# Seven products instead of eight for one more group of second products, with one block's products moved to the end

## The chip, the cores and the metric

One core of one Trainium2 chip runs the kernel. The metric is the time of the program on the device in microseconds (us), smaller being better. A profile of one execution tells, per engine, when each instruction began and how long it took.

## The reference, cut to what matters

```python
def chain(q, k, v, w_gate, w_val, w_out, rms_g, w_in, w_out2):   # names shortened
    a = decayed_linear_attention(q, k, v)      # 2 x 8 heads x 768 tokens x 64
    x = a.transpose(0, 2, 1, 3).reshape(1536, 512)
    xn = x / sqrt(mean(x * x, -1) + 1e-6) * rms_g
    g, val = xn @ w_gate, xn @ w_val           # 512 -> 1536
    x2 = (silu(g) * val) @ w_out               # 1536 -> 512   first layer
    h = x2 @ w_in                              # 512 -> 2048
    return maximum(0.01 * h, h) @ w_out2       # 2048 -> 512   second layer
```

The weights come as 64-bit floating point numbers and the rest in 32 bits.

## The kernel before, in words

**Data.** After the attention part the 1536 tokens lie in three blocks of 512 (0, 1, 2). Features run over the partitions in slabs of 128. The first layer has 12 slabs of hidden features, worked on in three groups of four (`G1`, groups 0 to 2); the second has 16, in four groups of four (`G2`, groups 3 to 6). A group makes its first products (`g` and `v`, or `i`), turns them into gated values, and multiplies these by its second weights (`o`, or `p`); the sums of the second products are kept across groups.

**A product** of fp32 accuracy is made of three products of rounded parts (high times high, high times low, low times high). So a slab's product with one block is 12 matmuls of 512 columns. Every value that enters a matmul needs a high part (a copy on ScalarE, ACT) and a low part (a subtraction on VectorE, DVE). A weight slab is first turned from 64-bit numbers into fp32 by four VectorE steps (L466, L470, L475, L484), then split (L487 on ACT, L491 on DVE).

**Sevens.** A pair of slabs and the blocks 1 and 2 form a two-by-two product. The kernel makes it with seven half products of sums and differences in place of eight. For the first products this is `quad` (7 steps of 6 matmuls, for a pair of slabs); for the second products it is `seventh`. It works on sums of gated values (`follow`, L741) and on sums of weights (L425, split at L432), and adds the result of each of the seven kinds to the kept sums with two VectorE additions (L807). The kinds run in the order 1, 5, 6, 3, 7, 2, 4. Block 0 is always multiplied plainly: `whole` for first products, `down` for second ones.

**Which groups.** `SEVEN = 4` names the four groups of the second layer, `SEVEN1 = (1,)` the first layer's middle group. In groups 0 and 2 the second products are plain: `down` for each slab and block, 12 matmuls each, and at a block's end `evac1` adds four banks to the kept sums.

**The kept sum of block 0** has no room in the fast memory while its tile (`extra()`, called `more` in the profile) holds gated values: `evac1` writes it with four GpSimd DMAs to `held` and, in group 1, reads it back with four more (L698).

**The turn to the second layer.** Group 2 ends with block 0, then block 1, then the four `down` steps of block 2. After a block the result is split into parts (`x2_parts`), and the sums over blocks 1 and 2 that the sevens of `i` need are made by `sums_of` (four differences, four high parts, four low parts, each over 1024 columns). These operations wait in the list `sums`, from which two are taken behind each step. `HEAD = "dddd0"` orders the beginning of group 3: four `down` steps, one `whole`, then the quads.

**Order and room.** `plan` writes the steps out in the order of TensorE; `run` walks them with a planner that gives VectorE and ACT assumed costs and puts weight conversions where it sees time, latest when a step needs the weight. Converted weight slabs take one of 14 places (`UNITS = 12` and `UNITS2 = 2`); a sum of two slabs takes two. A place is given back after the last product that reads it. Behind the hand-ordered attention part the framework orders each engine's queue by this order and by what is ready. Weights are loaded through SP's queue, three raw slabs ahead.

Of the kernel before, what the change touches and what calls it, by code (L numbers as in the profile page):

```python
# [8 lines left out]
F32 = mybir.dt.float32  # L9
# [3 lines left out]
AF = mybir.ActivationFunctionType  # L13
# [19 lines left out]
SEVEN1 = (1,)  # L33
HEAD = "dddd0"
# [29 lines left out]
def chain_kernel(ctx: ExitStack, tc: tile.TileContext, qk_t, kv, w1, w2, mask, qdec, kdec, sdec, rms_g, ident, out):  # L64
# [585 lines left out]
    def down(gi, f, b):  # L650
        kinds, fs = groups[gi]
        L = kinds[-1]
        key = (L, f, b)
        upper(key)
        lower(key)
        accumulate(L, gi, f, b, f == fs[0], f == fs[-1], L == "o" or b > 0)
        used(f"{L}{f}")
        if f == fs[-1]:
            banks = acc.pop("b")
            first = gi in (0, len(G1))  # L660
            by_copy = gi in (0, len(G1)) or b == 0 and gi not in (len(G1) - 1, len(groups) - 1)
            later.append(("a" if by_copy else "v", 2.4, lambda: (evac1 if L == "o" else evac2)(gi, b, banks)))
        placed[0] = order.index(key) + 1

    def evac1(gi, b, banks):
        last = gi == len(G1) - 1
        if b:
            if gi == 0:
                acc[b] = xp.tile([P, 4, 512], F32, tag=f"acc{b}", name=f"x2acc{b}")
            for m in range(4):  # L670
                dst = acc[b][:, m, :]
                if gi == 0:
                    nc.scalar.activation(out=dst, in_=banks[m], func=AF.Copy)
                else:
                    nc.vector.tensor_tensor(out=dst, in0=banks[m], in1=dst, op=ALU.add)
            if not last:
                return
            highs, lows = ([lambda m=m, do=do: do(m) for m in range(2 * b - 2, 4)] for do in x2_parts(b))
            if b == 1:
                sums.extend(highs + lows)  # L680
                return
            one, two = slice(0, 2), slice(2, 4)
            ops = sums_of(acc, x2h, x2l, acc[1][:, one], acc[1][:, two], x2h[2][:, one], x2l[2][:, one], extra()[:, two])
            both = [lambda i=i: [ops[n]() for n in (f"{i}", f"h{i}")] for i in range(4)]
            sums.extend(both[:2] + [ops["l1"]] + highs + [ops["l0"]] + lows + [both[2], ops["l2"], both[3], ops["l3"]])
            return
        acc[0] = extra()
        for m in range(4):
# [5 lines left out]
            if gi == 0:  # L694
                nc.gpsimd.dma_start(out=held[m], in_=t)
            else:
                nc.gpsimd.dma_start(out=held[m], in_=t, accum_op=ALU.add)
                nc.gpsimd.dma_start(out=t, in_=held[m])  # L698
        if last:
            high, low = x2_parts(0)  # L700
            sums.extend([lambda m=m, do=do: do(m) for do in (high, low) for m in range(4)])

# [53 lines left out]
    def seventh(gi, n, f):  # L756
# [44 lines left out]
        def put():  # L801
            for m in range(2):
# [3 lines left out]
                else:  # L806
                    nc.vector.tensor_tensor(out=dst, in0=banks[m], in1=dst, op=ALU.add)  # L807
            if gi == len(groups) - 1 and LAST[b, row] == n:
# [236 lines left out]
    def plan():  # L1045
# [12 lines left out]
        for gi, (kinds, fs) in enumerate(groups):  # L1058
# [19 lines left out]
            if first:  # L1078
                for n in HEAD:
                    if n == "d":  # L1080
                        fill.pop(0)()
                    else:
                        f = fs[int(n)]
                        put((f"i{f}",), lambda f=f: whole("i", f, 0, x2h, x2l))
# [9 lines left out]
            elif gi in seven:  # L1094
                for f in fs[::2]:
                    own = [fill.pop(0) for _ in range(min(2, len(fill)))]
# [4 lines left out]
                wholes = [lambda f=f: put((f"i{f}",), lambda: whole("i", f, 0, x2h, x2l)) for k, f in enumerate(fs) if not first or str(k) not in HEAD]  # L1101
# [241 lines left out]
```

## Time and profile before

| | |
|---|---|
| time, median of 3 runs | 580.07 us (580.04 to 580.52) |
| span of the profiled execution, first to last instruction | 578.7 us |
| busy TensorE (PE) / VectorE (DVE) / ScalarE (ACT) / GpSimd (POOL) | 569.6 / 516.4 / 361.8 / 39.3 us |
| matmuls | 3098 |

The profiled execution is told by its span; 1.4 us of the median lie outside it. An engine's busy time is the time in which at least one of its instructions ran. Instructions of one engine overlap in the profile: on VectorE an operation that is shown with 0.68 us can be followed 0.6 us after its start. L612 is line 612 of the kernel shown above.

### The profile page before, as it was taken

To read this page: it belongs to the slowest core of one execution; us is meant where nothing else is said; L and a number is where in the kernel's file an instruction comes from. 1 tells how busy PE (TensorE), PEld (TensorE's weight loads), DVE (VectorE), ACT (ScalarE), POOL (GpSimd) and SP (SyncE) were. 2 spreads that over 40 slices of the span, in tenths; PEclk is the share of its full clock that TensorE was granted. 3 is DMA by queue.
4 is the path that set the end of the run, shared out by engine and by line. 5 is a ranking of instruction groups with operands and counts; after the bars stand their busy time and mean duration, and the time that the engine had idled before them with its cause. 6 is when DMAs were issued, how large, how long until landed. Compare 5 with 4: busy or idle time off the path is not lost.

```text
span 578.7 us, 8510 instructions
## 1 busy us (share of the span) xinstructions
PE 569.6 (98%) x3098; PEld 470.1 (81%) x3098; DVE 516.4 (89%) x950; ACT 361.8 (63%) x666; POOL 39.3 (7%) x48
## 2 busy tenths in 40 slices
PE   8899999999999999999999999999999999999997
PEld 5788788887888888888888878888888888888886
DVE  5899999999577999999588999999999999997793
ACT  2789656776565455675464567778756785676330
POOL 2332100010000000030000000000100020002100
PEclk9999999999999999999999999999999999999999
DMA  8991240435022201484410111213511363011545
GB/s 336 408 386 61 74 143 3 143 117 178 1 72 74 72 2 36 117 199 170 133 57 18 37 36 37 72 40 108 182 37 37 109 151 73 33 36 24 123 81 139
DMA packets 34922, 60.13 MB, mean 104 GB/s; under 512 B 19392, under 2 KB 19776, under 8 KB 34880
## 3 DMA queue, kind: packets, MB, share of 16 engines
q1 hardware_dynamic: 31728, 52.24, 28.0%
q0 software_dynamic: 3008, 7.34, 5.5%
q8 instruction: 24, 0.39, 0.3%
q14 instruction: 18, 0.15, 0.1%
q10 hardware_dynamic: 144, 0.00, 0.0%
HBM read 51.19 MB, written 8.39 MB: 103 GB/s over the span
## 4 chain that ended last, share of the span: by engine, by line
PE 81%; DVE 8%; DMA 6%; ACT 3%; issue 1%; SPq 0%; POOL 0%; DVEq 0%; ACTq 0%; POOLq 0%
PE ao L612 10%; PE X L776 9%; PE iX L974 8%; PE ap L612 8%; PE i L581 8%; PE Z L776 7%; PE v L581 6%; PE g L581 6%; PE gX L974 4%; PE iZ L974 4%; PE vX L974 4%; PE gZ L974 2%; DMA qkv<-in_qk_t 2%; PE vZ L974 2%; PE iY L974 2%; DMA qkv<-in_kv 2%
## 5 line engine op out<-in xcount | busy, mean ns | idle before, releaser
L612 PE MATMUL ap<-w_p,gp_0h 128*128 128x512 f32 (+1 forms) x130 | 39.6, 386 | 0.0
L581 PE MATMUL i<-x2h,w_i 128*128 128x512 f32 x128 | 31.8, 390 | 0.0
L581 PE MATMUL g<-xh,w_g 128*128 128x512 f32 x128 | 31.8, 391 | 0.0
L581 PE MATMUL v<-xh,w_v 128*128 128x512 f32 x128 | 31.7, 390 | 0.0
L612 PE MATMUL ao<-go_0h,w_o 128*128 128x512 f32 x96 | 31.5, 390 | 0.0
L612 PEld LDWEIGHTS ap<-w_p,gp_0h 128*128 128x128 f32 x130 | 24.4, 188 | 5.0
L581 PEld LDWEIGHTS g<-xh,w_g 128*128 128x128 f32 x128 | 24.0, 188 | 5.1 <-issue 0.2
L581 PEld LDWEIGHTS i<-x2h,w_i 128*128 128x128 f32 x128 | 24.0, 188 | 5.0
L581 PEld LDWEIGHTS v<-xh,w_v 128*128 128x128 f32 x128 | 24.0, 188 | 4.9
L612 PE MATMUL ap<-w_p,gp_0l 128*128 128x512 f32 (+1 forms) x65 | 25.1, 386 | 0.0
L912 ACT ACTIVATE more<-i 128x512 f32<-128x512 f32 x16 | 9.5, 594 | 21.5 <-PE i L581 21.5
L612 PEld LDWEIGHTS ao<-go_0h,w_o 128*128 128x128 f32 x96 | 18.0, 188 | 3.7
L612 PE MATMUL ao<-go_2h,w_o 128*128 128x512 f32 x64 | 20.6, 391 | 0.1
L612 PE MATMUL ao<-go_1h,w_o 128*128 128x512 f32 x64 | 20.4, 390 | 0.0
L974 PE MATMUL iZ<-x2h,w_si 128*128 128x512 f32 x64 | 20.3, 391 | 0.0
L974 PE MATMUL iX<-th,w_si 128*128 128x512 f32 x64 | 19.8, 391 | 0.0
L612 PE MATMUL ao<-go_0l,w_o 128*128 128x512 f32 x48 | 18.7, 389 | 0.0
L538 ACT ACTIVATE wb_i<-raw_i 128x512 int32<-128x512 uint32 x16 | 10.8, 673 | 11.2 <-DVE wa_p L484 3.9
L581 PE MATMUL v<-xl,w_v 128*128 128x512 f32 x64 | 17.2, 392 | 0.0
L581 PE MATMUL g<-xl,w_g 128*128 128x512 f32 x64 | 17.2, 391 | 0.0
L197 DVE TENSOR_TENSOR a<-sc,mask_sb 128x1024 f32<-128x1024 f32 (+1 forms) x13 | 14.6, 1137 | 3.0 <-PE sc L185 2.6
L581 PE MATMUL i<-x2l,w_i 128*128 128x512 f32 x64 | 17.1, 390 | 0.0
(366 smaller groups left out, 1776.5 us busy)
## 6 DMA issues: line engine op xcount, KB each, us to landing
raw_i<-in_w SPq DMA_DIRECT2D x16, 512.0 KB, 3.8
raw_p<-in_w SPq DMA_DIRECT2D x16, 512.0 KB, 3.7
raw_g<-in_w SPq DMA_DIRECT2D x12, 512.0 KB, 4.1
raw_v<-in_w SPq DMA_DIRECT2D x12, 512.0 KB, 3.8
raw_o<-in_w SPq DMA_DIRECT2D x12, 512.0 KB, 3.6
qkT<-in_qk_t SPq DMA_DIRECT2D x7, 512.0 KB, 6.6
kv<-in_kv SPq DMA_DIRECT2D x7, 512.0 KB, 8.1
out<-more POOLq DMA_DIRECT2D x12, 256.0 KB, 4.2
```

Source lines behind the costliest of these rows:

```text
L197: nc.vector.tensor_tensor(out=s["a"][:, j], in0=s["sc"][:, j], in1=mask_sb[:, j], op=ALU.mult)
L538: nc.scalar.activation(out=m, in_=low.bitcast(U32), func=AF.Copy, scale=2.0 ** -29)
L581: nc.tensor.matmul(out=dst, lhsT=lhs, rhs=rhs, start=(n == 0), stop=(n == len(pairs) - 1), skip_group_check=True)
L612: nc.tensor.matmul(out=acc["b"][m][:, c:c + cut], lhsT=lhs, rhs=rhs[:, c:c + cut], start=(start and n == 0), stop=(stop and n == 2), skip_ ...
L776: nc.tensor.matmul(out=acc[side][m], lhsT=lhs, rhs=rhs, start=(start and f == fs[0] and k == 0), stop=(f == fs[-2] and k == 2), skip_group ...
L912: nc.scalar.activation(out=a, in_=x, func=AF.Prelu, alpha=0.01)
L974: nc.tensor.matmul(out=dst, lhsT=lhs, rhs=rhs, start=(start and n == 0), stop=(n == 5), skip_group_check=True)
```

## The change

The second products of group 2 are made as sevens too (`SEVEN1 = (1, 2)`), for blocks 1 and 2. Their weights `o8` to `o11` are converted behind all of the group's `g` and `v`, and two pairs of weight sums are made for them. Block 0's gated values of the group go into `extra()`, so the kept sum stays in `held` one group longer: the read-back of its slab m moves out of `evac1` into `down`, behind the making of the parts of the slab that lay there. Block 0's four `down` steps come behind the sevens, and then the quads of `i` begin without a `whole` ahead of them; block 0's four `whole` steps of group 3 go two into its second quad and two among its sevens. The parts of blocks 1 and 2 and their sums are taken up as soon as the last of the seven kinds for a half of a block is added (`x2_sums`, called from `seventh`); `sums_of` is called without a spare tile.

```diff
--- before.py
+++ after.py
@@ -30,8 +30,7 @@
 COST_SUM = {n: ("a", 0.54) if n in "Hh" else ("v", 0.34 if n in "1234" else 0.6) for n in "123H4hLl"}
 TWICE = "gvi"
 SEVEN = 4
-SEVEN1 = (1,)
-HEAD = "dddd0"
+SEVEN1 = (1, 2)
 RAWS = 3
 WARM = 7
 LOADS = "q0 k0 m g s k1 q1 d q2 q3 k2 k3 q4 k4 q5 w w q6 w q7 k6 k8 k7 k5 i q8 q9 k9 q10 k10"
@@ -653,6 +652,9 @@
         key = (L, f, b)
         upper(key)
         lower(key)
+        if gi == len(G1) - 1:
+            m = f - fs[0]
+            nc.gpsimd.dma_start(out=extra()[:, m, :], in_=held[m])
         accumulate(L, gi, f, b, f == fs[0], f == fs[-1], L == "o" or b > 0)
         used(f"{L}{f}")
         if f == fs[-1]:
@@ -665,24 +667,9 @@
     def evac1(gi, b, banks):
         last = gi == len(G1) - 1
         if b:
-            if gi == 0:
-                acc[b] = xp.tile([P, 4, 512], F32, tag=f"acc{b}", name=f"x2acc{b}")
+            acc[b] = xp.tile([P, 4, 512], F32, tag=f"acc{b}", name=f"x2acc{b}")
             for m in range(4):
-                dst = acc[b][:, m, :]
-                if gi == 0:
-                    nc.scalar.activation(out=dst, in_=banks[m], func=AF.Copy)
-                else:
-                    nc.vector.tensor_tensor(out=dst, in0=banks[m], in1=dst, op=ALU.add)
-            if not last:
-                return
-            highs, lows = ([lambda m=m, do=do: do(m) for m in range(2 * b - 2, 4)] for do in x2_parts(b))
-            if b == 1:
-                sums.extend(highs + lows)
-                return
-            one, two = slice(0, 2), slice(2, 4)
-            ops = sums_of(acc, x2h, x2l, acc[1][:, one], acc[1][:, two], x2h[2][:, one], x2l[2][:, one], extra()[:, two])
-            both = [lambda i=i: [ops[n]() for n in (f"{i}", f"h{i}")] for i in range(4)]
-            sums.extend(both[:2] + [ops["l1"]] + highs + [ops["l0"]] + lows + [both[2], ops["l2"], both[3], ops["l3"]])
+                nc.scalar.activation(out=acc[b][:, m, :], in_=banks[m], func=AF.Copy)
             return
         acc[0] = extra()
         for m in range(4):
@@ -695,10 +682,28 @@
                 nc.gpsimd.dma_start(out=held[m], in_=t)
             else:
                 nc.gpsimd.dma_start(out=held[m], in_=t, accum_op=ALU.add)
-                nc.gpsimd.dma_start(out=t, in_=held[m])
         if last:
             high, low = x2_parts(0)
             sums.extend([lambda m=m, do=do: do(m) for do in (high, low) for m in range(4)])
+
+    x2_ops = {}
+
+    def x2_sums(b, row):
+        one, two = slice(0, 2), slice(2, 4)
+        high, low = x2_parts(b)
+        ms = range(2 * row, 2 * row + 2)
+        own = [lambda m=m, do=do: do(m) for do in (high, low) for m in ms]
+        if b == 2 and not row:
+            return []
+        if b == 2:
+            return own
+        if not row:
+            x2_ops.update(
+                sums_of(acc, x2h, x2l, acc[1][:, one], acc[1][:, two], x2h[2][:, one], x2l[2][:, one])
+            )
+        both = [lambda i=i: [x2_ops[n]() for n in (f"{i}", f"h{i}")] for i in range(4)]
+        lows = [lambda i=i: x2_ops[f"l{i}"]() for i in range(4)]
+        return own + (both[3:] + lows[3:] if row else both[:3] + [lows[2], lows[0], lows[1]])
 
     def x2_parts(b):
         if b not in x2h:
@@ -805,6 +810,8 @@
                     nc.scalar.activation(out=dst, in_=banks[m], func=AF.Copy)
                 else:
                     nc.vector.tensor_tensor(out=dst, in0=banks[m], in1=dst, op=ALU.add)
+            if gi == len(G1) - 1 and LAST[b, row] == n:
+                sums.extend(x2_sums(b, row))
             if gi == len(groups) - 1 and LAST[b, row] == n:
                 t = units.tile([P, 2, 16, 32], F32, tag="u", name=f"turned{b}_{row}")
                 for m in range(2):
@@ -1076,12 +1083,8 @@
             fill = downs(groups[gi - 1][1], 0 if gi - 1 in seven else 2, gi - 1) if gi else []
             first = gi == len(G1)
             if first:
-                for n in HEAD:
-                    if n == "d":
-                        fill.pop(0)()
-                    else:
-                        f = fs[int(n)]
-                        put((f"i{f}",), lambda f=f: whole("i", f, 0, x2h, x2l))
+                while fill:
+                    fill.pop(0)()
             if gi in seven and L == "o":
                 wholes = [lambda n=n, f=f: put((f"{n}{f}",), lambda: whole(n, f, 0, xh, xl)) for f in fs for n in kinds[:-1]]
                 for f in fs[::2]:
@@ -1092,13 +1095,15 @@
                             if i7 in BEHIND[2] and own:
                                 own.pop(0)()
             elif gi in seven:
+                wholes = [lambda f=f: put((f"i{f}",), lambda: whole("i", f, 0, x2h, x2l)) for f in fs]
                 for f in fs[::2]:
+                    if first and f > fs[0]:
+                        fill, wholes = wholes[:2], wholes[2:]
                     own = [fill.pop(0) for _ in range(min(2, len(fill)))]
                     for i7, (keys, step) in enumerate(quad("i", f)):
                         put(keys, step)
                         if i7 in BEHIND[2] and own:
                             own.pop(0)()
-                wholes = [lambda f=f: put((f"i{f}",), lambda: whole("i", f, 0, x2h, x2l)) for k, f in enumerate(fs) if not first or str(k) not in HEAD]
             if gi in seven:
                 for n, more in zip((1, 5, 6, 3, 7, 2, 4), (1, 0, 1, 0, 1, 0, 1)):
                     for f in fs[::2]:
```

## Rows read from the trace of the kernel before

**Rows 1.** The page, busy time of each engine over the span, instructions behind the x.
```profile
PE 569.6 (98%) x3098; PEld 470.1 (81%) x3098; DVE 516.4 (89%) x950; ACT 361.8 (63%) x666; POOL 39.3 (7%) x48
```
**Rows 2.** The page, VectorE's busy tenths in 40 slices of 14.5 us.
```profile
DVE  5899999999577999999588999999999999997793
```
**Rows 3.** Waits of TensorE over the span: total us, times, longest (longest row).
```profile
PE sc L185 <- DMA qkv<-in_qk_t: 2.3, 3, 1.0
```
**Rows 4.** The chain from 290 us: start, us, what.
```profile
300.83 2.72 PE ao L612 x12
```
**Rows 5.** Timeline of TensorE at the turn of blocks 1 and 2: start, us, instruction.
```profile
323.56 0.39 PE L612 MATMUL ao<-go_1h,w_o 128*128 128x512 f32 x1
324.08 0.47 PE L612 MATMUL ao<-go_2h,w_o 128*128 128x512 f32 x1
```
**Rows 6.** VectorE's groups by shape, 315 to 337 us: count, busy us, mean ns.
```profile
L675 DVE TENSOR_TENSOR x2acc<-ao,x2acc 128x512 f32<-128x512 f32 x8 | 5.1, 686 | 0.0
```
**Rows 7.** The same view, 174 to 232 us, the first layer's second group.
```profile
L807 DVE TENSOR_TENSOR x2acc<-X,x2acc 128x512 f32<-128x512 f32 x8 | 5.2, 682 | 0.0
L807 DVE TENSOR_TENSOR x2acc<-Z,x2acc 128x512 f32<-128x512 f32 x6 | 4.0, 684 | 0.0
...
L432 DVE TENSOR_TENSOR w_so<-wa_o,w_so 128x512 fp32r<-128x512 f32 x4 | 2.7, 684 | 0.0
L425 DVE TENSOR_TENSOR wa_o<-wa_o,wa_o 128x256 f32<-128x256 f32 x6 | 2.5, 420 | 0.1
...
L741 DVE TENSOR_TENSOR gs<-gs,gs 128x512 f32<-128x512 f32 x2 | 1.4, 688 | 0.0
```
**Rows 8.** Timeline of VectorE around the second layer's first sevens.
```profile
358.73 0.42 DVE L425 TENSOR_TENSOR wa_p<-wa_p,wa_p 128x256 f32<-128x256 f32 x1
359.06 0.68 DVE L741 TENSOR_TENSOR is<-iu,is 128x512 f32<-128x512 f32 x1
359.67 0.42 DVE L425 TENSOR_TENSOR wa_p<-wa_p,wa_p 128x256 f32<-128x256 f32 x1
...
363.73 0.68 DVE L432 TENSOR_TENSOR w_sp<-wa_p,w_sp 128x512 fp32r<-128x512 f32 x1
```
**Rows 9.** Busy time of VectorE by stretch: stretch and length, busy (instructions).
```profile
234.00:255.00 21.00, 20.52 (x43) 1.00 0.58 153
255.00:364.50 109.50, 97.05 (x169) 1.00 0.24 77
364.50:421.00 56.50, 56.31 (x108) 1.00 0.31 103
421.00:520.00 99.00, 97.95 (x187) 1.00 0.25 70
```
**Rows 10.** Timeline of TensorE, first product of the sevens' third kind, group 3.
```profile
365.25 0.39 PE L776 MATMUL X<-gq_6h,w_sp 128*128 128x512 f32 x1
```
**Rows 11.** Timeline of VectorE, the last weight sum of group 4.
```profile
419.79 0.69 DVE L432 TENSOR_TENSOR w_sp<-wa_p,w_sp 128x512 fp32r<-128x512 f32 x1
```
**Rows 12.** Timeline of TensorE, the same third kind of product, group 4.
```profile
422.37 0.39 PE L776 MATMUL X<-gq_6h,w_sp 128*128 128x512 f32 x1
```
**Rows 13.** VectorE's groups by shape, 404 to 420.3 us.
```profile
L475 DVE SCALAR_TENSOR_TENSOR wa_i<-raw_i,wa_i 128x512 int32<-128x512 int32 x2 | 1.4, 684 | 0.0
...
L470 DVE TENSOR_SCALAR wa_i<-wa_i 128x512 int32<-128x512 int32 x2 | 0.8, 420 | 0.0
L466 DVE TENSOR_SCALAR wa_i<-wa_i 128x512 f32<-128x512 f32 x2 | 0.8, 419 | 0.0
...
L484 DVE CUSTOM_DVE_ANT_0 wa_i<-wa_i,wb_i 128x1024 uint16<-128x1024 uint16 x1 | 0.7, 683 | 0.0
```
**Rows 14.** Timeline of TensorE, first product with the weights of group 5.
```profile
444.13 0.62 PE L974 MATMUL iX<-x2h,w_i 128*128 128x512 f32 x2
```
**Rows 15.** Timeline of VectorE, in brackets the idle time before and its releaser.
```profile
288.63 0.69 DVE L922 TENSOR_TENSOR g<-v,g 128x512 f32<-128x512 f32 x1 [6.08 <-PE v L581]
```
**Rows 16.** Timeline of TensorE, start of the products of the first layer's last group.
```profile
231.31 0.61 PE L974 MATMUL gX<-xh,w_g 128*128 128x512 f32 x2
```
**Rows 17.** Timeline of GpSimd, the first read-back of a kept sum.
```profile
256.89 0.58 POOL L698 DMA_DIRECT2D more<-held  x1 [2.74 <-DVE wa_o L470]
```
**Rows 18.** DMA issues: count, KB each, median us from issue to landing.
```profile
more<-held POOLq DMA_DIRECT2D x4, 256.0 KB, 5.4
```

## Prediction

> **What bounds the kernel now.** I read the page first. TensorE is busy for 98% of the span and VectorE for 89% [rows 1]; but the slices show VectorE at 9 tenths from about 300 to 520 us with hardly a break [rows 2]. Two engines are near their limit, so the next view is who waits. TensorE's list of waits is short: five entries, the largest of 2.3 us in three pieces, all at lines of the attention part [rows 3]. In the two layers TensorE simply runs: twelve matmuls take 2.72 us [rows 4], 0.2267 us each, and the same step shows everywhere. The one visible hitch near the change is at the turn from block 1 to block 2: two matmuls that should start 0.23 us apart start 0.52 us apart [rows 5], so 0.3 us is lost.
>
> So the time is the number of matmuls, as long as VectorE keeps up. How near it is to not keeping up is read in two ways. First its idle time: 0.5 us in 234 to 255 us, 12.45 us in 255 to 364.5, 0.2 us in 364.5 to 421, and 1.05 us in the 99 us after that [rows 9]. Second, how long before its use a weight is ready. The last weight sum for group 3's sevens ends at 364.4 us [rows 8]; the product that needs it is in the second half of the kind that starts at 365.25 [rows 10], and it reads the low part eight matmuls later, at 367.1. The lead is 2.7 us. In group 4 the last one ends at 420.5 [rows 11] and is needed at 422.37 + 1.81 = 424.2 [rows 12], a lead of 3.7 us.
>
> **The change part by part.**
>
> *Matmuls.* Plain, blocks 1 and 2 cost 4 slabs x 2 blocks x 12 = 96 matmuls; as sevens 2 pairs x 7 x 6 = 84. Twelve go: -2.7 us [rows 4]. The turn from block 1 to block 2 goes too, and its hitch with it: -0.3 us [rows 5]. That is -3.0 us on the engine that sets the end.
>
> *VectorE.* What it does more of is seen in group 1, which works this way already. Its price per operation is the distance of two starts, 0.33 us for 256 columns and 0.61 us for 512 [rows 8]; the shown durations, 0.42 and 0.68, would count the overlap twice. Weight sums: eight of 256 columns and four low parts [rows 7], 8 x 0.33 + 4 x 0.61 = 5.1 us. Low parts of the gated sums: 14 in place of 8, 3.7 us. Differences at L741: 4 per pair, 8 in all, the line in [rows 7] standing for four such lines of two: 4.9 us. Additions to the kept sums: 14 [rows 7] in place of 8 [rows 6], 3.7 us. Together 17.3 us (19.8 if the durations counted). Block 0's additions, x2's parts and the sums over blocks are as many as before.
>
> *ACT.* Six more high parts and four for weight sums; it is busy for 361.8 us of 578.7 [rows 1] and hides them.
>
> *Where VectorE can put 17.3 us.* The idle time from 234 to 364.5 us is 12.9 us, to 421 us 13.1 us [rows 9]. If all of it can be used, group 3's last weight sum comes 17.3 - 12.9 = 4.4 us later, at 368.8, while TensorE wants it at 367.1 - 0.3 = 366.8 (the twelve matmuls saved are spent on one more `whole` ahead of this point): 2.0 us late. Group 4's comes 4.2 us later, at 424.7, and is wanted at 424.2 - 3.0 = 421.2: 3.5 us late. But not all that stands ahead of it is as urgent: before it VectorE had already done seven steps on the weights of group 5 [rows 13], 4 x 0.33 + 3 x 0.61 = 3.2 us, and these are first used at 444.13 [rows 14]. If they give way, 0.3 us of stall is left. So the stall is between 0.3 and 3.5 us. I take 1.0, nearer the low end, because those seven steps are for later weights and the order of work follows the order of need.
>
> *Idle time that can't be used.* Of the 12.9 us, 6.1 us is one wait [rows 15], ending with a product of TensorE: VectorE had run ahead as far as the 14 places let it. After the change the second weights and their sums hold eight places through the sevens, and four more are held by slabs that wait for a `whole`, so only two are free for layer 2 as the sevens begin. In exchange there is more of other work there: low parts, differences and additions. The unusable part lies between 0 and 6.1 us. I take 1.0, as most of that hole is filled by the sums for the second weights, which are wanted right then.
>
> *Moves.* The four `down` steps of block 0 (48 matmuls, 10.9 us) now stand where the parts and sums over blocks 1 and 2 must be made, and ask little of VectorE: four low parts and four additions. That is the cover for the 9 to 13 us of VectorE work at the turn; without it, it would stall TensorE. `HEAD`'s `whole` only changes places. The weights come through SP in another order within the group, and each is fetched three ahead as before: nothing. The read-backs keep their number; GpSimd has nothing else to issue there.
>
> The sum: -3.0 + 1.0 + 1.0 = -1.0 us, against the profiled execution 577.7 for its 578.7 us of span; 1.4 us lie outside, so against the median 580.07 the time is **579.1 us**.
>
> **The rivals.**
>
> *All hidden.* VectorE's urgent work always goes first and its spare time reaches. For it: group 1 did the same with VectorE full and no wait of TensorE; leads of 2.7 and 3.7 us [rows 8, 10 to 12]. Against it: at group 4 the lag is larger than the lead. Time: 580.07 - 3.0 = 577.0.
>
> *Slower: no place to convert into.* From 231.3 us [rows 16] the new order has 264 matmuls (quads, block 0 of group 1, four `whole`) to the first seven, which begins at 231.3 + 59.9 = 291.2. Until two `whole` of the seven kinds' stretch are through, 60 matmuls or 13.6 us later (304.8), two slots for the next weight sum aren't free. VectorE's other work there is some 18 operations of 0.61 us, 11 us, so up to 2.6 us is idle. Four weight sums and six slabs must then be made between 304.8 and 366.8: 4 x 2.54 + 6 x 2.49 = 25 us, beside some 40 us of parts, sums and additions, 65 us in 62. With the idle time, and if group 5's steps don't give way, group 4's sum is 3.5 + 2.6 = 6.1 us late: 580.07 - 3.0 + 6.1 = 583.2. It decides as soon as lateness passes 4.2 us. For it: [rows 15] is this very wait.
>
> *The read-back is late.* Block 0's last `down` begins at 231.3 + 432 x 0.2267 = 329.2 us; if its parts are made just then, the read takes 0.6 us to issue and 5.4 us to land [rows 17, 18], to 335.2, while the addition that needs it is due after three others at 332.0 + 1.8 = 333.8. VectorE then stands 1.4 us, or 4.1 us if GpSimd waits 2.7 us first, as it did [rows 17]; some of this comes on top: about 581. Against it: parts were made two steps ahead wherever VectorE had time.
>
> The Trainium skill bears on that issue: the page "SBUF — State Buffer", section "SBUF: two separate sides", says that GpSimd can't write a DMA's descriptors while VectorE runs an operation that takes both of its ports. The row agrees in the name it gives (the wait ended with VectorE's L470) but not in size, since one such operation takes 0.42 us [rows 13] and the wait was 2.74 us [rows 17]. By the rule alone one issue waits 0.4 us at most, and the time would be 579.5.
>
> **How the numbers follow.** The forecast has a chance of 0.40, with its own range of 578.0 to 580.3; all hidden 0.29; no place to convert into 0.21; the late read-back 0.10. What a measurement of this kernel can tell is about 0.2%, 1.16 us: faster is below 578.9, slower above 581.2. Faster: all hidden, and the lower part of the forecast's own range, 0.29 + 0.15 = 0.44. Same: the rest of the forecast and 0.04 of the read-back, 0.29. Slower: 0.21 + 0.06 = 0.27. The range reaches from the first rival to just short of the second, 576.9 to 583.0.
>
> **What would show it.** 3086 matmuls. VectorE at 9 tenths from 230 us on, with hardly an idle microsecond between 255 and 421, and about 17 us more of starts. TensorE's waits, if any, before sevens of groups 3 and 4 and on weight sums (L432) or low parts (L635), 2 us or less in all; no wait at the start of group 3's quads. If the hole of 6 us returns, now around 290 to 305, the second rival is right; if VectorE waits at L691 for a DMA, the third. The prediction is wrong if VectorE stays idle and TensorE still waits, or if the priorities put later weights first and the stall passes 4 us.

## The result and the profile after

The changed kernel takes 586.07 us (median of 4 runs, 584.63 to 586.70), against 580.06 us (579.95 to 580.52) of the kernel before, run beside it: a ratio of 1.010, 95% interval 1.0085 to 1.0114. The forecast of 579.1 us and its range miss it, on the slow side. The profiled execution has a span of 584.5 us. Line numbers have shifted: L424, L431 and L490 below are L425, L432 and L491 of the kernel before, L465 to L483 the conversion steps L466 to L484, L427, L486, L536 and L580 are L428, L487, L537 and L581, L781 is L776, L981 is L974 and L998 is L991.

The page of the changed kernel, for [rows 1] and [rows 2], and the granted clock in 40 slices:

```profile
PE 571.7 (98%) x3086; PEld 467.1 (80%) x3086; DVE 532.7 (91%) x982; ACT 368.1 (63%) x676; POOL 39.6 (7%) x48
...
DVE  5899999998677999997999998999999999999893
...
PEclk9999999999999999999999998999999999999999
```

Twelve matmuls are gone and VectorE has 32 operations and 16.3 us more, as counted beforehand. New is an 8 in the clock's row. The list of TensorE's waits, of which the kernel before had none in the layers [rows 3], from 250 to 420 us (total us, times, longest):

```profile
PE iZ L981 <- ACT w_si L427: 2.6, 1, 2.6
PE iX L981 <- ACT iu L998: 0.7, 1, 0.7
PE iX L981 <- ACT w_i L486: 0.5, 1, 0.5
```

All three lie in the first two quads of the second layer. The timeline of TensorE around the largest (start, us, instruction, in brackets the idle time before):

```profile
346.54 0.39 PE L981 MATMUL iY<-x2l,w_i 128*128 128x512 f32 x1
349.50 0.50 PE L981 MATMUL iZ<-x2h,w_si 128*128 128x512 f32 x1 [2.57 <-ACT w_si L427]
...
351.82 0.63 PE L981 MATMUL iZ<-x2l,w_si 128*128 128x512 f32 x1
352.24 0.63 PE L981 MATMUL iX<-th,w_si 128*128 128x512 f32 x1
352.67 1.48 PE L580 MATMUL i<-x2h,w_i 128*128 128x512 f32 x3
```

and its busy time in four stretches (the number behind the bracket is the granted clock, 1.00 being full speed):

```profile
335.00:346.70 11.70, 10.36 (x42) 1.00 0.14 46
346.70:349.50 2.80, 0.23 (x2) 1.00 0.51 184
349.50:354.50 5.00, 5.00 (x15) 0.66 0.31 105
354.50:364.50 10.00, 10.00 (x46) 1.00 0.02 5
```

TensorE waits for the weight sum si2 of `i2` and `i3`, the second pair of group 3, and afterwards runs eight matmuls 0.40 to 0.43 us apart, nearly twice the 0.227 of [rows 4]: the gap costs its length and then 1.6 us of half clock, 1.2 in place of 2.4 GHz. Adding up, over the layers, by how much more than 0.227 us the starts of consecutive matmuls lie apart (only distances above 0.235 us are counted) gives 1.0 us for the kernel before and 9.5 us here, 6.9 of it from 330 to 360 us. 8.5 more less 2.7 for the twelve matmuls is 5.8, and the spans differ by 584.5 - 578.7 = 5.8: this is the whole loss.

Why si2 is late is seen on VectorE and ACT. Of VectorE, the first step of `i3` (L465), the low parts of `i2` and `i3` (L490) and the first low part of si2:

```profile
339.82 0.42 DVE L465 TENSOR_SCALAR wa_i<-wa_i 128x512 f32<-128x512 f32 x1
340.15 0.68 DVE L490 TENSOR_TENSOR w_i<-wa_i,w_i 128x512 fp32r<-128x512 f32 x1
...
346.31 0.68 DVE L490 TENSOR_TENSOR w_i<-wa_i,w_i 128x512 fp32r<-128x512 f32 x1
...
349.48 0.69 DVE L431 TENSOR_TENSOR w_si<-wa_i,w_si 128x512 fp32r<-128x512 f32 x1
```

`i2` and `i3` are split at 340.8 and 347.0 us; in the kernel before the same was done at 302.8 and 315.7, and si2 at 318.9, 30 us ahead of its use at 348.9. VectorE's busy time by stretch, for [rows 9]:

```profile
140.00:180.00 40.00, 27.11 (x51) 1.00 0.27 79
180.00:234.00 54.00, 50.82 (x93) 1.00 0.10 30
234.00:255.00 21.00, 20.81 (x44) 1.00 0.45 130
255.00:290.00 35.00, 30.86 (x58) 1.00 0.46 118
290.00:335.00 45.00, 44.37 (x71) 1.00 0.12 36
335.00:364.50 29.50, 27.15 (x52) 0.94 0.16 55
```

From 290 to 335 us VectorE is full. What isn't converted when the sevens begin (288 to 291 us) comes behind them and behind x2's parts. So the question for the runs is: is it the amount of VectorE work, its place, the order of the work at the turn, or something that kept these weights from being converted earlier?

### The profile page after: what moved, and what is told of

The parts are those of the page before. It is cut to its first block, busy times and chain, and to the rows that moved or that the text cites. A ratio compares the mean times of both kernels' runs of the same rounds, so it can differ in the third digit from the quotient of the medians.

```text
span 584.5 us, 8533 instructions
## 1 busy us (share of the span) xinstructions
PE 571.7 (98%) x3086; PEld 467.1 (80%) x3086; DVE 532.7 (91%) x982; ACT 368.1 (63%) x676; POOL 39.6 (7%) x48
## 4 chain that ended last, share of the span: by engine, by line
PE 80%; DVE 9%; DMA 6%; ACT 2%; issue 1%; SPq 0%; POOL 0%; DVEq 0%; ACTq 0%; POOLq 0%
PE X L781 11%; PE Z L781 8%; PE i L580 8%; PE ap L611 7%; PE iX L981 7%; PE ao L611 7%; PE v L580 6%; PE g L580 6%; PE gX L981 4%; PE vX L981 4%; PE iZ L981 3%; PE gZ L981 2%; DMA qkv<-in_qk_t 2%; PE vZ L981 2%; PE iY L981 2%; DMA qkv<-in_kv 2%
## 5 line engine op out<-in xcount | busy, mean ns | idle before, releaser
L580 PE MATMUL i<-x2h,w_i 128*128 128x512 f32 x128 | 33.4, 395 | 0.0
L580 PE MATMUL g<-xh,w_g 128*128 128x512 f32 x128 | 31.8, 390 | 0.0
L580 PE MATMUL v<-xh,w_v 128*128 128x512 f32 x128 | 31.7, 390 | 0.0
L580 PEld LDWEIGHTS i<-x2h,w_i 128*128 128x128 f32 x128 | 24.5, 191 | 5.2
L580 PEld LDWEIGHTS g<-xh,w_g 128*128 128x128 f32 x128 | 23.9, 188 | 5.2 <-issue 0.2
L580 PEld LDWEIGHTS v<-xh,w_v 128*128 128x128 f32 x128 | 23.9, 188 | 5.0
L981 PE MATMUL iZ<-x2h,w_si 128*128 128x512 f32 x64 | 21.0, 400 | 2.6 <-ACT w_si L427 2.6
L981 PE MATMUL iX<-th,w_si 128*128 128x512 f32 x64 | 22.0, 410 | 0.8 <-ACT iu L998 0.7
L196 DVE TENSOR_TENSOR a<-sc,mask_sb 128x1024 f32<-128x1024 f32 (+1 forms) x13 | 14.5, 1135 | 3.0 <-PE sc L184 2.9
L580 PE MATMUL v<-xl,w_v 128*128 128x512 f32 x64 | 17.2, 391 | 0.0
L580 PE MATMUL g<-xl,w_g 128*128 128x512 f32 x64 | 17.2, 391 | 0.0
L580 PE MATMUL i<-x2l,w_i 128*128 128x512 f32 x64 | 17.1, 389 | 0.0
L981 PEld LDWEIGHTS iX<-th,w_si 128*128 128x128 f32 x64 | 12.1, 192 | 6.1 <-ACT iu L998 1.5
L981 PEld LDWEIGHTS iZ<-x2h,w_si 128*128 128x128 f32 x64 | 12.1, 189 | 6.1 <-ACT w_si L427 3.1
L812 DVE TENSOR_TENSOR y2acc<-X,y2acc 128x512 f32<-128x512 f32 x26 | 16.9, 681 | 0.0
```

Of the source, the lines that this page charges most:

```text
L196: nc.vector.tensor_tensor(out=s["a"][:, j], in0=s["sc"][:, j], in1=mask_sb[:, j], op=ALU.mult)
L580: nc.tensor.matmul(out=dst, lhsT=lhs, rhs=rhs, start=(n == 0), stop=(n == len(pairs) - 1), skip_group_check=True)
L981: nc.tensor.matmul(out=dst, lhsT=lhs, rhs=rhs, start=(start and n == 0), stop=(n == 5), skip_group_check=True)
```

## The experiments

Each was timed beside the kernel before (580.2 to 580.4 us); "lost" is TensorE's time beyond 0.227 us per matmul, as above. The first of them rest on the theory that the amount of VectorE work decides.

**32 idle VectorE operations of 448 columns in the kernel before.** Nothing reads their result.

```diff
+    def spin():
+        nc.vector.tensor_tensor(out=idle_tile, in0=idle_tile, in1=idle_tile, op=ALU.max)
...
```

> The kernel before with 32 idle VectorE operations (448 columns, 0.53 us each, 17 us together, on a tile that nothing reads) spread behind the steps of the first layer's last group; nothing else is changed, the matmuls are as many and the output is the same. Theory 'amount' (VectorE's added work does not fit before the last weights of group 3 are due): 17 us less 12.9 us of idle time less the lead of 2.7 us is 1.4 us at the least, and as the changed kernel lost 9 us where it should have saved 3, 3 to 9 us more: 583 to 589 us, with waits of TensorE between 330 and 370 us. Theory 'order' (the work would fit, but in the changed kernel the second pair's quad comes right behind the first's and later weights stand ahead of its own): at most 1 us more, 580 to 581 us.

597.90 us, ratio 1.0295 (1.0277 to 1.0312). It misses its aim: with no input from the layers the operations ran at 1.8 to 49.5 us, in the attention part, and the layers lost 1.1 us, as without them (1.0). Next, 36 of them with an input from block 0's kept sum:

> The kernel before with idle VectorE operations of 448 columns that wait for the kept sum of the first layer's second group, so that 28 of 36 of them (14.9 us) stand among VectorE's work of the last group; matmuls and output as before. In the first run of this kind the idle operations depended on nothing and ran in the attention part. Theory 'amount': 14.9 us against 12.9 us of idle time (of which 2 to 4 us can't be used) and 2.7 us of lead: 1 to 4 us slower, 581.4 to 584.4 us, with waits of TensorE on weights between 335 and 375 us. Theory 'arrangement' (what is lost is lost by putting block 0 last, not by VectorE's work): within 0.6 us of before.

589.68 us, 1.016 (1.0145 to 1.0175), and flawed as well: one operation stood 6.9 us for a DMA and held all that was queued behind it on VectorE.

```profile
DVE spin L1257 <- DMA more<-held: 6.9, 1, 6.9
```

The third reads block 1's kept sum instead, and so runs without a wait.

```diff
+    def spin(k):
+        src = acc[1][:, 0, :448] if k % 4 == 3 else spin_tile
+        nc.vector.tensor_tensor(out=spin_tile, in0=src, in1=src, op=ALU.max)
...
     def run(i, keys, b, step, behind):
...
+        if int(keys[0].lstrip("sgvoip")) >= 9 and keys[0].lstrip("s")[0] in "gvo" and spins[0]:
+            spins[0] -= 1
+            later.append(("v", 0.53, lambda k=spins[0]: spin(k)))
```

> The kernel before with 32 idle VectorE operations of 448 columns that read the kept sum of block 1 (ready before the first layer's last group begins), all among VectorE's work of that group: in the earlier run they had waited for a DMA and held VectorE for 6.9 us. They take 32 x 0.53 = 17 us; matmuls and output as before. Amount: the changed kernel lost 9 us beside the 3 it saved, but with 2.7 to 4 us of it at the lower clock; here 4 to 9 us slower than before, 584 to 589 us, with VectorE idle for less than 6 us from 255 to 364 us. Places (it is the places held by the second weights and their sums): the work goes into the idle time, at most 2 us slower.

581.09 us, 1.0013 (1.0000 to 1.0025). Where they ran, and VectorE's busy time:

```profile
L1257 DVE TENSOR_TENSOR spin<-spin x24: 617/622/632, 233.4 to 293.7; 128x448 f32<-128x448 f32 x24
L1257 DVE TENSOR_TENSOR spin<-x2acc x8: 617/622/627, 232.2 to 289.7; 128x448 f32<-128x448 f32 x8
```
```profile
255.00:276.00 21.00, 20.89 (x42) 1.00 0.55 158
276.00:290.00 14.00, 14.00 (x28) 1.00 0.33 112
```

20 us more of VectorE work at 232 to 294 us cost 0.9 us: the amount as such fits, if it can go where VectorE is idle.

**The changed kernel with less VectorE work.** First without the eight differences of the new sevens and the eight 256-column sums of `o8` to `o11` (left out, 7.5 us); then without all 17 us (also the new low parts and six additions; of the weight sums' low parts ACT makes a copy).

```diff
             def combine(out, in0, in1, op):
+                if n == "o" and f >= 8:
+                    return lambda: None
...
         def less(out, in0, in1):
+            if q == "r" and f >= 8:
+                return
```

> The changed kernel without eight of its additional VectorE operations of 512 columns (the differences of gated values in group 2) and without the eight of 256 columns that form the sums of group 2's second weights: 4.9 + 2.6 = 7.5 us of VectorE's work is left out, so the second products of that group are not the reference's; the order of all else stays. Amount: the lost time between 332 and 355 us falls from about 8 us to under 1.5 us and the clock stays at its upper level: 577.5 to 579.5 us. Order: the waits stay nearly whole: 584 us or more.

583.32 us, 1.0048 (1.0033 to 1.0064): the waits at 330 to 355 us are gone, and 2.7 us of 6 are back; a sum of the `p` weights is waited for in their place (1.2 us).

> The changed kernel without all of its additional VectorE work: the eight differences, the eight and four operations for the sums of second weights (ACT makes four plain copies in their place), six of fourteen low parts and six of fourteen additions in group 2: 17 us are left out, and the group's second products are not the reference's. Matmuls, places, order and lead-over are those of the changed kernel. Amount: the saving appears, 577 us (576.5 to 578.2). Places: 2 us of waits at group 3's sevens stay, 579 to 581 us.

579.19 us, 0.9980 (0.9966 to 0.9993); no wait of TensorE from 250 to 420 us is left. So the added VectorE work, with all that hangs on it, costs the 7 us, and the matmuls saved are worth what they should be: the span falls by 1.1 us, 2.7 less 1.6 more lost in small waits. Whether it is the amount of work, this run doesn't tell: the weight sums that were left out also let go of their tiles sooner, and ACT copies `i2` and `i3` into theirs at 288.3 and 291.1 us, where the changed kernel has 293.9 and 297.9:

```profile
288.34 0.67 ACT L542 ACTIVATE wa_i<-raw_i 128x512 f32<-128x512 f32 x1
...
291.06 0.68 ACT L542 ACTIVATE wa_i<-raw_i 128x512 f32<-128x512 f32 x1
```

**The arrangement without the work**: block 0 last, its read-back in `down`, no `HEAD`, but group 2's second products plain (`SEVEN1 = (1,)`), and the sums over blocks made by the first step of a quad at the latest.

> One part of the change alone: group 2's second products plain (96 matmuls for blocks 1 and 2, as before, block 2 first), but with the group's order, its weights' order, block 0 last, the kept sum held longer and the new lead-over. VectorE's work is that of before. Amount: no time is lost to VectorE, 579.5 to 581.5 us. Arrangement: the waits between 330 and 355 us appear here too, 583 us or more.

580.79 us, 1.0018 (0.9996 to 1.0041): a difference that can't be told from none.

**Order at the turn.** Two of block 0's `whole` between the two quads; and the low parts of a weight sum straight behind its high parts. The first run of the latter named si12 and si14, which are group 6's (the second layer counts its slabs from 0), so it tells nothing of the turn (586.89 us); the second names si0 and si2.

```diff
-                        fill, wholes = wholes[:2], wholes[2:]
+                        while len(wholes) > 2:
+                            wholes.pop(0)()
```
```diff
+            if key in ("si0", "si2"):
+                converting.extend(tails)
+                tails.clear()
```

> The changed kernel with the two whole products of block 0 put between the first and the second quad of group 3, and not inside the second: the same work, but 5.4 us of matmuls stand ahead of the second pair's weights. Amount: the wait moves to the weights of group 3's sevens, and only the clock's fall (about 1.5 us) is saved: 584 to 585.5 us. Order: the wait of 2.6 us goes, and the clock's fall with it, and it does not come back: 580.5 to 582.5 us.

584.45 us, 1.0069 (1.0054 to 1.0084): the wait moves to a sum of the `p` weights at 370 us, and 1.6 us are won.

```profile
PE X L781 <- ACT w_sp L427: 2.3, 1, 2.3
```

> The changed kernel with the low parts of group 3's two sums of first weights put directly behind their other steps, ahead of the first steps of the second weights: the same work, in the order of need for these two. Amount: within 1 us of the changed kernel, 585 to 587 us. Order, in the form 'later weights' steps stand ahead': 3.5 us of such steps go behind, the wait of 2.6 us goes and the clock stays up: 582 to 583.5 us.

> The changed kernel, but the low parts of the weight sums of the second layer's first group (si0 and si2; an earlier run did this with si12 and si14, which belong to its last group, and so told nothing of the turn) are queued at once behind their high parts instead of behind the next weight's steps. In the changed kernel seven steps of p0 and p1 (about 3.5 us of VectorE) stand before si2's low parts at 341 to 349 us. Theory 'amount times place': VectorE is full there, so what goes first delays the rest: 584 to 587 us, the wait moves from 349.5 us to others. Rival 'the order of these low parts': the wait of 2.6 us and the clock's fall behind it go: 581.5 to 583.

586.39 us, 1.0107 (1.0085 to 1.0128), the wait of 2.6 us unmoved. The order of these parts isn't it.

**Places.** 15 in place of 14, paid with a raw buffer (`UNITS2 = 3`, `RAWS = 2`); then 13 (`UNITS2 = 1`) in either kernel.

> The changed kernel with 15 places for converted weights in place of 14, paid for with a raw slab (two ahead in place of three). Theory 'places' (VectorE stands idle around 260 to 290 us because no place is free, and lacks that time later): idle time from 255 to 330 us falls from 4.3 us by 2 us or more, and 1.5 to 3 us are won: 583 to 584.5 us. Theory 'amount': idle time is a matter of when data come; within 1 us of the changed kernel, 585 to 587 us; if loads come late, more.

607.79 us, 1.048 (1.046 to 1.050). Some 16 us went ahead of the layers (the same matmul starts at 91.6 us in place of 75.9), as there is a raw buffer less; but at the turn the same waits stand, with one place more:

```profile
PE iZ L981 <- ACT w_si L427: 2.7, 1, 2.7
```

> The changed kernel with 13 places for converted weights in place of 14. Places: VectorE stands idle longer around 260 to 290 us, and 2 to 4 us are lost beside the changed kernel: 588 to 590 us. Amount: within 1 us of the changed kernel.

586.09 us, 1.0096 (1.0065 to 1.0127), as with 14.

> The kernel before with 13 places in place of 14, the counterpart. Places: it has 12 us of idle time to give, so it loses less than the changed kernel does by the same step: at most 1.5 us more than before, 580 to 581.5 us. If it loses as much as the changed kernel, a place costs by itself and says nothing of the change.

580.22 us, 0.9989 (0.9970 to 1.0008). So the 14 places don't bind.

**Part of the work on GpSimd.** A first run moved the differences and all weight sums from `o8` on, the whole second layer's among them, far more than meant; the second only the eight differences.

```diff
-            nc.vector.tensor_tensor(out=out, in0=in0, in1=in1, op=ALU.subtract)
+            (nc.gpsimd if q == "r" and f >= 8 else nc.vector).tensor_tensor(out=out, in0=in0, in1=in1, op=ALU.subtract)
```

> The changed kernel with the eight differences of gated values of group 2 and the sums of weights from group 2's second ones to group 3's last (24 operations of 256 columns) on GpSimd: the output is the reference's, 4.9 + 7.9 = 12.8 us leave VectorE. GpSimd's 512-column product in the attention part took 1.3 us, so these take about 26 us of an engine with nothing else to do there. Amount: nearly all lost time goes, 577.5 to 580 us. Places: about 2 us of waits stay at group 3's sevens, as in the run with less VectorE work, 581 to 583 us. If GpSimd's latency in the chain of a weight sum decides: 584 us or more.

617.37 us, 1.0627 (1.0602 to 1.0653): GpSimd's sums come late all along.

> The changed kernel, with the eight differences of gated values that the new sevens need (8 x 0.6 = 4.9 us of VectorE, 512 columns) on GpSimd, where one took 1.3 to 2.0 us in an earlier run; nothing else moved. Theory 'amount times place': 4.9 us less for VectorE in front of the turn gives back about as much per microsecond as leaving out 7.5 us did (2.7 us less than the changed kernel), if the differences still come in time: 583.5 to 585.5 us. Rival 'the differences are late': the sevens wait for GpSimd, 587 us or more. Rival 'amount is not it': 586 as before.

585.95 us, 1.0098 (1.0083 to 1.0113). The wait at 349 us is gone, but the sevens wait for a difference instead (1.1 us, up to 303.8 us), and a quad of `g` stands 1.5 us, up to 265.4 us. Nothing is won.

**The same amount right in front of the turn.** The 32 idle operations again in the kernel before, now behind the low part of `i0`.

```diff
+        src = wt["i0"][:, 0, :448].bitcast(F32) if k % 4 == 3 else spin_tile
...
+        if "i0" in wt:
+            for _ in range(min(2, spins[0])):
+                spins[0] -= 1
+                later.append(("v", 0.53, lambda k=spins[0]: spin(k)))
```

> The kernel before with 32 idle VectorE operations of 448 columns added (0.62 us each as the earlier run with the same operations showed, 19.8 us in all), as in the run that had them all at 232 to 294 us, but in VectorE's order they now stand behind the low part of the second layer's first weight i0 (282.6 us in the kernel before), most of them before the turn to the second layer; no other operation uses what they write. Theory 'amount times place': VectorE work is only dear right in front of the turn. From 282.6 to 335 us the kernel before has about 9 us of VectorE idle time, so some 8 to 11 us are carried into the turn, where x2's parts, its sums and the weights i0 to i3 and their sums wait in the same queue: 583 to 588 us, TensorE waits of 3 us or more in 330 to 375 us, on weights or parts of x2. Rival 'the chain of the new operations' (the sevens' own dependencies make the wait, not how much VectorE has to do there): 581.5 or less, hardly a wait more than with the same operations earlier (581.1).

582.20 us, 1.0033 (1.0020 to 1.0046), with no wait of TensorE from 250 to 420 us large enough for the list; 2.4 us lost.

```profile
L1257 DVE TENSOR_TENSOR spin<-spin x24: 610/617/626, 283.1 to 350.0; 128x448 f32<-128x448 f32 x24
L1257 DVE TENSOR_TENSOR spin<-w_i x8: 610/617/626, 282.4 to 331.7; 128x448 f32<-128x448 f32 x8
```

Neither number came. Amount and place, without the other buffers that the new work holds, explain 2 of 6 us: here `i0` to `i3` and si2 were ready at 282 to 322 us as before, and what slid was `p1` (331.2 to 351.3 us), which could afford it. So the theory fell in this form. What remained was why, in the changed kernel, weights of group 3 come that late.

**Letting conversions run ahead.** In every step the planner may place conversions up to 8 us ahead of TensorE's plan, in place of 1.5 us when they are behind.

```diff
-        limit = clock["pe"] + (OVER if behind else 0.0)
+        limit = clock["pe"] + 8.0
```

> The changed kernel, but the emitter lets conversions of weights run up to 8 us of VectorE and ScalarE time ahead of TensorE's plan in every step (before: 1.5 us, and only when it is behind), so that the weights of the second layer's first group stand earlier in VectorE's order and the idle time left at 255 to 285 us (about 4 us) can be used. Theory 'amount times place': there are only some 4 us of idle time left there, and the sevens' own work is pushed later instead: 583 to 587 us, the wait of 2.6 us at 349.5 us gone or smaller but others in its place. Rival 'the plan holds the weights back': the waits of 330 to 355 us go and nothing comes in their place: 577.5 to 580.

583.40 us, 1.0057 (1.0040 to 1.0073): 2.7 us won. The second half of si0 is ready at 316.0 us in place of 338.1, two of the three waits go, and in the profiled execution the granted clock stays at 1.00; but `i3` and si2 are hardly sooner (344.6 and 348.0 us in place of 347.0 and 350.2):

```profile
PE iZ L981 <- ACT w_si L427: 2.3, 1, 2.3
```

**The buffers ahead of a conversion.** A weight under conversion lies in one of four staging tiles (`stage_a`, `wa` in the rows), and a pair that is to be summed keeps two of them until its sums are split. Group 2's `o` pairs are new among these. In the changed kernel the low parts of the weight sums of `o8`, `o10` and `i0` on VectorE (`so8`'s at 276.37 us, two in one row):

```profile
276.37 1.28 DVE L431 TENSOR_TENSOR w_so<-wa_o,w_so 128x512 fp32r<-128x512 f32 x2
...
292.59 0.68 DVE L431 TENSOR_TENSOR w_so<-wa_o,w_so 128x512 fp32r<-128x512 f32 x1
...
296.80 0.68 DVE L431 TENSOR_TENSOR w_so<-wa_o,w_so 128x512 fp32r<-128x512 f32 x1
...
337.41 0.68 DVE L431 TENSOR_TENSOR w_si<-wa_i,w_si 128x512 fp32r<-128x512 f32 x1
```

and ACT's copies of the next weights into staging tiles (`i0` and `i1`, `i2`, `i3`, `p1`):

```profile
277.08 1.28 ACT L536 ACTIVATE wa_i<-raw_i 128x512 f32<-128x512 f32 x2
...
293.89 0.66 ACT L536 ACTIVATE wa_i<-raw_i 128x512 f32<-128x512 f32 x1
...
297.93 0.67 ACT L536 ACTIVATE wa_i<-raw_i 128x512 f32<-128x512 f32 x1
...
338.12 0.68 ACT L536 ACTIVATE wa_p<-raw_p 128x512 f32<-128x512 f32 x1 [0.35 <-DVE w_si L431]
```

Each copy comes within 0.7 us behind the low part that ends a tile's use, and for the last one the row names it; before the others ACT was busy, so their rows name nothing. On this reading `i2` and `i3` can't begin before 293.9 and 297.9 us, when the sevens run and VectorE is full; it gets to `i3` at 339.82. Another buffer showed up too: at 268 to 270.5 us ACT waits 2.5 us for the raw data of `i1`, with high parts of `o` queued behind. The last two runs take these apart, both with conversions running ahead and paid with one of the 14 places: a fourth raw buffer, or six staging tiles.

```diff
+        pools["a"] = ctx.enter_context(tc.tile_pool(name="stage_a2", bufs=2))
...
-        a = stage_a.tile([P, 512], F32, tag="a", name=f"wa_{key}")
+        pair = [key for key, x in wq if x is not None].index(key) // 2
+        a = (pools["a"] if "a" in pools and pair % 3 == 2 else stage_a).tile([P, 512], F32, tag="a", name=f"wa_{key}")
...
```

> The kernel with conversions running ahead (583.4 us), with a fourth buffer for raw weights behind the attention in exchange for one of the 14 places (one place less cost nothing in an earlier run). In both kernels ScalarE stands at 267 to 271 us for the raw data of the second weight of the second layer (2.5 us, 3.3 us with running ahead), with o10's and o11's high parts queued behind that copy, and VectorE then idles 2.4 to 2.9 us; of 35 us from 255 to 290 VectorE is idle 4.1 us (5.6 with running ahead). Theory 'the idle time in front of the sevens is locked by the buffers ahead of the conversions': VectorE idles 2 to 3 us less there, i0 to i3 are ready 2 to 3 us sooner, the wait of 2.3 us at 347 us mostly goes: 580.5 to 582.5. Rival 'what is full behind 290 us decides alone': 583 to 584 us, the wait at 347 us stays over 1.5 us.

583.96 us, 1.0057 (1.0042 to 1.0072): ACT's wait for raw data is gone, TensorE's 2.3 us stay. The raw data isn't it.

> As the run before, but instead of the raw buffer two more staging buffers (six instead of four) for weights under conversion, which a pair of weights holds until its sums are made; in the changed kernel i0's first step starts at 277.8 us right behind the high parts of o8's weight sums (276.6), and i2's at 298.7 behind those of o10's (294.0). Theory 'locked by the staging buffers': i0 to i3 start earlier, VectorE idles 2 us or more less in 255 to 290 us, 580.5 to 582.5. Rival: the raw data or the full time behind 290 us decide: 583 to 584 us.

579.57 us, 0.9992 (0.9982 to 1.0001): the loss is gone, and no wait of TensorE from 250 to 420 us is left. `i2`'s and `i3`'s first steps, and si2:

```profile
276.72 0.42 DVE L465 TENSOR_SCALAR wa_i<-wa_i 128x512 f32<-128x512 f32 x1
...
277.52 0.42 DVE L465 TENSOR_SCALAR wa_i<-wa_i 128x512 f32<-128x512 f32 x1
...
343.26 0.68 DVE L431 TENSOR_TENSOR w_si<-wa_i,w_si 128x512 fp32r<-128x512 f32 x1
```

They stood at 298.67 and 339.82 us; now all four steps of both are made by 281.9 us, ahead of the sevens, and si2 comes 6 us earlier. Where VectorE found the time:

```profile
140.00:180.00 40.00, 31.08 (x58) 1.00 0.33 102
180.00:234.00 54.00, 51.39 (x94) 1.00 0.09 32
234.00:255.00 21.00, 20.83 (x43) 1.00 0.42 139
255.00:290.00 35.00, 30.61 (x58) 1.00 0.44 112
```

Not in the idle time at 255 to 290 us, which stays at 4.4 us (4.1 in the changed kernel), but 100 us earlier: up to 255 us VectorE has done 103.3 us of work since 140 us in place of 98.7. Of these 4.6 us, 4.0 went into the stretch from 140 to 180 us, where VectorE idles 12.9 us in the changed kernel. Running ahead with four tiles doesn't do this: up to 255 us it gives 99.0 us of work, and 99.3 with the raw buffer.

## Why the prediction was wrong

*Matmuls, hitch, VectorE's amount, ACT.* Right: 3086 matmuls; the hitch at the turn of blocks 1 and 2 [rows 5] is gone; 32 more VectorE operations and 16.3 us more busy time for the 17.3 us of starts; 6.3 us more on ACT. The run with all of the added work left out fits the 2.7 us for the matmuls, with 1.6 lost elsewhere. ACT, though, doesn't hide everything: it stood 2.5 us for raw data (up to 270.5 us) with high parts queued behind.

*Where VectorE can put the work.* This is a step that failed. It took the last weight sums of groups 3 and 4 as the first to come late. What came late was the second pair of group 3's first weights, which had 30 us of lead and was never looked at, and the waits came in the quads, where the prediction expected none at the start; the sum of p's second pair, at 364.4 us in [rows 8], came at 374.7 without a wait of its own. A lead in time says nothing when the conversion can't begin: the pair lost its lead because it stood behind the sums of two new pairs, and with six tiles, running ahead, the wait is gone.

*Idle time that can't be used.* The term that was mis-sized: with the stall above it was 2.0 us, and 8.5 were lost, 1.6 of them to the clock. It looked at the 14 places alone; these don't bind (13 and 15 changed nothing at the turn). The four staging tiles do, together with how far the planner lets conversions run ahead. The rival "no place to convert into" had the right kind of mechanism at the wrong buffer, and its 583.2 us was still 2.9 us short. The budget was also cut too late: it began at 234 us, but most of the idle time that paid for the cure lies at 140 to 180 us, and with running ahead it was the number of weights that may be under conversion at once that decided whether it could be used.

*Moves.* Right: block 0's `down` steps cover x2's parts without a wait, and the arrangement alone costs 0.18% (-0.04 to 0.41).

*The late read-back.* This rival did not come: the read-backs were issued between 318 and 327 us, and VectorE waits for no DMA between 288 and 345 us. The 2.74 us of [rows 17] were also misread. Most of that wait was for the slab's own write to `held`, which was issued at 250.35 us and landed at 256.3; so the row says little about VectorE standing in GpSimd's way, and in the changed kernel those writes were issued 59 us or more ahead of the reads.

*The clock.* Not foreseen: 1.6 of the 8.5 us come from the clock that fell behind the 2.57 us gap.

Two things stay open: what six staging tiles give without running ahead (that pair wasn't taken apart), and what keeps 4.4 us of VectorE idle at 255 to 290 us. From the same matmul near 90 us to the start of the last one the version with six staging tiles takes 482.75 us and the kernel before 484.5, but behind that matmul come 4.76 us in place of 4.07, so that little is left of the gain; no version here beats the kernel before by a difference that could be told from none, except the one that leaves work out.

## What to carry to other kernels

A busy engine's spare time is only worth what the buffers in front of its work let it reach: before adding work to it, list every tile that the work must hold (places, raw data, staging), for how long, and compare the number of pairs in flight before and after. Look at the lead of every piece that is made behind the new work, not only of the tightest one. The Trainium skill, page "Perfetto Trace Analysis", section "Optimization Strategy", says that the same gap coming again and again on the engine that should be saturated can mean that there is no room for the next tile; here the sign was another one, since VectorE was full (44.4 of 45 us) where it hurt and idle 100 us before.

## What the runs showed of the hardware

One gap of TensorE of 2.57 us was followed, 1.5 us after it resumed, by eight matmuls, seven of them 0.427 us apart (granted clock 0.66 from 349.5 to 354.5 us). Gaps of 2.3 us went either way: behind the one in the run with two `whole` between the quads the clock fell too (0.51 from 371.7 to 375.2 us), behind the one in the kernel with conversions running ahead it stayed at 1.00. Of the four runs of the changed kernel, the one whose mean clock was 1.000 was the fastest, 584.6 us; the others had 0.996 to 0.997 and 585.9 to 586.7 us. The Trainium skill, page "TensorE: Matmul & The Clock Gate", section "Wait — 56ns, not 53.3ns?", gives 426.7 ns from start to start for 512 columns at the low clock; the trace agrees (0.427 us).

GpSimd took 0.78 to 1.11 us for a 256-column sum and 1.29 to 2.04 us for a 512-column one, means of the groups in the run that moved both:

```profile
L424 POOL TENSOR_TENSOR wa_i<-wa_i 128x256 f32<-128x256 f32 x16 | 17.8, 1113 | 89.4 <-DVE w_i L490 69.0 <-ACT more L919 12.3 <-ACT go_0h L626 7.5
...
L424 POOL TENSOR_TENSOR wa_p<-wa_p 128x256 f32<-128x256 f32 x8 | 6.3, 784 | 0.6
...
L746 POOL TENSOR_TENSOR gs<-gu,gs 128x512 f32<-128x512 f32 x2 | 4.1, 2037 | 0.0
...
L746 POOL TENSOR_TENSOR gs<-gs,gs 128x512 f32<-128x512 f32 x2 | 2.6, 1292 | 11.3 <-DVE gr_5l L634 11.3
```

VectorE's operations of the same shapes are shown with 0.42 and 0.68 us [rows 8]. The Trainium skill, page "GPSIMD Engine Reference", section "Engine selection", says about twice VectorE's time for two inputs; these rows give 1.9 to 3.0 times, and GpSimd's times are rough in the profile.
